# Longer runs for the q and k loads, and a new count of filler products, in an attention-then-GLU kernel

## Chip, cores, metric

One NeuronCore of one Trainium2 chip. The metric is the device time of one execution in microseconds (us), the median of several; lower is better.

## The reference, cut

```python
qn = q / (norm(q, axis=1) + 1e-6); kn = k / (norm(k, axis=1) + 1e-6)   # q, k, v: [4, 6016, 256] f32
a  = softmax(kn.transpose(0, 2, 1) @ qn / tau)                          # [4, 256, 256]
x  = (v @ a).reshape(24064, 256)
out = (sigmoid(x @ w_gate) * (x @ w_val)) @ w_out                       # d_ff = 1536
```

"Head" here means one of the four batch entries. Its 256 x 256 attention matrix needs all of its q and k before anything can be done with v.

## The kernel before

Each head has 6016 rows, 47 per partition. The kernel folds the attention matrix into the weights (`gh`: G = a @ w_gate, H = a @ w_val), so v only has to be transposed and multiplied by G and H. While the PE does this for one head, the q and k of the next are loaded, squared and scored as side work. Only head 0 has nothing to hide behind. All q, k, v and weights are cast from f32 to bf16 by the DMA and issued by POOL, in one queue (q0 in the profile); the transposes of v and the stores of the output are issued by SP, in another (q1). A chunk of v is four rows per partition, like a group of q and k; its products with G and H come in twelve slots. A filler product is one whose result nobody reads.

```python
TPC = 4                                  # rows per partition in one load
groups = [(0, 4), (4, 4), ..., (40, 4), (44, 3)]
qkpool = pool("qkpool", NCH)             # 12 buffers of 4 rows, for q and for k

def load_qk(b, t0, nt):
    for name, src in (("q", q), ("k", k)):
        tl = qkpool.tile([P, TPC, C], BF16, tag=name, name=name + "_sb")
        nc.gpsimd.dma_start(out=tl[:, :nt, :], in_=rows(src, b)[:, t0 : t0 + nt, :])
    ...
# head 0: rows 0-3 as f32 through SP and ACT, then load_qk for 4-7, 8-11, ..., 40-43, 44-45, 46,
# then v chunk 0, three pieces each of w_gate and w_val, v chunk 1, w_out
for g, (t0, nt) in enumerate(groups0):   # head 0
    ...                                  # squares on DVE and ACT, sums on DVE
    for u in range(nt):
        score(0, t0, u)
    if g < n_acc:                        # n_acc = 9: rows 0 to 35
        busy(5)                          # filler products: nobody reads their result
    ...                                  # norm products
# side work for head n, in slots of one 128-wide part of the hidden layer, 12 to a chunk of v
for g, (t0, nt) in enumerate(groups):
    s0 = first + g * (last - first) // NCH
    at(max(0, s0 - 20), load_qk, n, t0, nt)
    ...
# v of chunk ci + 2 is loaded at slot 0 of chunk ci, chunk ci + 1 is transposed at slot 2:
nc.sync.dma_start_transpose(out=vT[:, : nt * CB, :], in_=flat)   # chunks 0 and 1 of head 0: on the PE
```

## Time and profile before

| | before |
|---|---|
| time | 831.2 us (830.94 to 831.69, 6 runs) |
| PE busy | 816.1 us of a span of 829.0 |
| transfers on the chain that ended last | up to 37.3 us, then none |
| loads of q, k | 96, of 128 packets of data each |

The page gives the busy time of each engine and the chain of work that ended last. As the PE is busy 98% of the time, the chain is what to read: it says that only the first 37 us are set by something else. The lines are in the prediction.

### The profile page before, as it was taken

How to read it: one execution, taken by the hardware profiler on the slowest of the kernel's cores; microseconds unless marked ns; L12 is line 12 of the kernel's file. 1: busy time of each engine (PE TensorE's matmuls, PEld its weight loads, DVE VectorE, ACT ScalarE, POOL GpSimd, SP SyncE). 2: the span in 40 equal slices, each digit the busy share in tenths (PEclk: the TensorE clock that was granted, in tenths of full speed). 3: DMA queues.
4: the chain of work that ended last, by engine and by line, in shares of the span. 5: the costliest groups of instructions: out<-in, count | busy, mean ns of one | idle time of the engine just before them, and what ended most of it. 6: DMA issues, size and time to landing. Idle time of an engine off the chain costs nothing.

```text
span 829.0 us, 13765 instructions
## 1 busy us (share of the span) xinstructions
PE 816.1 (98%) x5192; PEld 502.6 (61%) x5206; DVE 588.9 (71%) x1022; ACT 391.6 (47%) x644; POOL 83.1 (10%) x159
## 2 busy tenths in 40 slices
PE   7899999999999999999999999999999999999998
PEld 4556666665665666665575666666566566666666
DVE  6577777887667777778767777777766666666664
ACT  4654444446644444445654444444655444444442
POOL 5531100002120100000211010000000000000000
PEclk9999999999999999999999999999999999999999
DMA  9999623226946433223875352223323423322111
GB/s 209 207 206 207 113 52 86 57 60 131 159 87 124 96 85 60 57 52 84 156 140 126 81 105 59 51 63 75 64 62 63 72 52 87 67 48 73 43 36 71
DMA packets 78739, 77.17 MB, mean 93 GB/s; under 512 B 50769, under 2 KB 55633, under 8 KB 78673
## 3 DMA queue, kind: packets, MB, share of 16 engines
q0 software_dynamic: 23920, 38.81, 28.3%
q1 hardware_dynamic: 54608, 36.97, 17.6%
q8 instruction: 40, 0.66, 0.3%
q10 hardware_dynamic: 144, 0.52, 0.2%
q14 instruction: 27, 0.21, 0.1%
HBM read 78.64 MB, written 24.64 MB: 125 GB/s over the span
## 4 chain that ended last, share of the span: by engine, by line
PE 94%; DMA 4%; DVE 1%; issue 0%; POOL 0%; ACT 0%; POOLq 0%; ACTq 0%
PE ps_o L88 30%; PE ps_gate L88 29%; PE ps_val L88 29%; PE ps_s L88 4%; DMA q_sb<-in_q_dram 3%; PE ps_gh L88 2%; DMA w_val<-in_moe_w_val_dram 1%; DVE hT L423 0%; ACT g_sb L422 0%; DVE sq L176 0%; PE ps_n L88 0%; POOL k_sb L97 0%; POOL q_sb L97 0%; PE ps_tp L393 0%; DVE out_sb L449 0%
## 5 line engine op out<-in xcount | busy, mean ns | idle before, releaser
L423 DVE TENSOR_TENSOR hT<-ps_val,g_sb 128x512 bf16<-128x512 f32 (+1 forms) x576 | 391.2, 680 | 206.3 <-ACT g_sb L422 201.9
L422 ACT ACTIVATE g_sb<-ps_gate 128x512 bf16<-128x512 f32 (+1 forms) x576 | 338.1, 588 | 386.0 <-PE ps_gate L88 380.0
L88 PE MATMUL ps_gate<-vT,gh_G 128*128 128x512 bf16 (+1 forms) x1152 | 337.6, 375 | 0.6 <-ACT g_sb L422 0.4
L88 PE MATMUL ps_val<-vT,gh_H 128*128 128x512 bf16 (+1 forms) x1152 | 337.4, 375 | 0.4
L88 PE MATMUL ps_o<-w_out_sb,hT 128*128 128x256 bf16 x2256 | 326.2, 273 | 0.0
L88 PEld LDWEIGHTS <-hT 128*128 128x128 bf16 x2256 | 220.7, 98 | 124.8
L88 PEld LDWEIGHTS <-gh_H 128*128 128x128 bf16 x1152 | 112.7, 98 | 131.6 <-issue 1.4
L88 PEld LDWEIGHTS <-gh_G 128*128 128x128 bf16 x1152 | 112.4, 98 | 38.5 <-issue 0.6
L106 POOL DMA_DIRECT2D v_sb<-in_v_dram x48 | 25.6, 533 | 619.9 <-DMA vT<-v_sb 485.8
L449 DVE COPY out_sb<-ps_o 128x256 f32<-128x256 f32 x188 | 77.9, 414 | 13.5 <-PE ps_o L88 13.5
L88 PE MATMUL ps_s<-k_sb,q_sb 128*128 128x256 bf16 x376 | 66.0, 272 | 5.7 <-DMA k_sb<-in_k_dram 4.3
L88 PEld LDWEIGHTS <-q_sb 128*128 128x128 bf16 x376 | 36.6, 98 | 14.1 <-issue 6.3
L215 DVE TENSOR_TENSOR acc<-acc,sq 128x1024 bf16<-128x1024 bf16 (+1 forms) x66 | 44.2, 669 | 0.0
L176 DVE TENSOR_TENSOR sq<-q_sb 128x1024 bf16<-128x1024 bf16 (+2 forms) x44 | 29.4, 668 | 2.7 <-DMA q_sb<-in_q_dram 2.7
L97 POOL DMA_DIRECT2D k_sb<-in_k_dram x48 | 26.3, 549 | 16.5 <-DMA k_sb<-in_k_dram 8.9
L97 POOL DMA_DIRECT2D q_sb<-in_q_dram x48 | 26.2, 545 | 16.0 <-DMA q_sb<-in_q_dram 8.6
L176 DVE TENSOR_TENSOR sq<-k_sb 128x1024 bf16<-128x1024 bf16 (+2 forms) x34 | 22.4, 658 | 0.9 <-ACT sq L174 0.9
L376 ACT ACTIVATE gh_G<-ps_gh,rrow 128x512 bf16<-128x512 f32 x21 | 14.4, 687 | 12.7 <-PE ps_gh L88 8.8
L174 ACT ACTIVATE sq<-k_sb 128x1024 bf16<-128x1024 bf16 (+1 forms) x11 | 11.2, 1018 | 14.6 <-DMA k_sb<-in_k_dram 11.8
L88 PE MATMUL ps_busy<-ones_wide,ones_bf 128*128 128x512 bf16 x57 | 16.3, 412 | 1.7 <-DVE shift L127 1.6
L378 DVE TENSOR_SCALAR gh_H<-ps_gh,rrow 128x512 bf16<-128x512 f32 x22 | 16.4, 743 | 1.6 <-PE ps_gh L88 1.6
L472 DVE TENSOR_TENSOR acc<-acc,sq 128x1024 bf16<-128x1024 bf16 x16 | 11.1, 692 | 5.1 <-ACT sq L174 4.8
(65 smaller groups left out, 124.5 us busy)
## 6 DMA issues: line engine op xcount, KB each, us to landing
out_dram<-out_sb SPq DMA_DIRECT2D x44, 512.0 KB, 2.9
v_sb<-in_v_dram POOLq DMA_DIRECT2D x44, 256.0 KB, 3.8
q_sb<-in_q_dram POOLq DMA_DIRECT2D x43, 256.0 KB, 7.8
k_sb<-in_k_dram POOLq DMA_DIRECT2D x43, 256.0 KB, 8.5
out_dram<-out_sb SPq DMA_DIRECT2D x4, 384.0 KB, 2.5
w_gate<-in_moe_w_gate_dram POOLq DMA_DIRECT2D x3, 256.0 KB, 6.8
w_val<-in_moe_w_val_dram POOLq DMA_DIRECT2D x3, 256.0 KB, 7.4
w_out_sb<-in_moe_w_out_dram POOLq DMA_DIRECT2D x1, 768.0 KB, 12.6
```

The source lines that it names most:

```text
L88: nc.tensor.matmul(out, lhsT=lhsT, rhs=rhs, start=start, stop=stop, **kw)
L97: nc.gpsimd.dma_start(out=tl[:, :nt, :], in_=rows(src, b)[:, t0 : t0 + nt, :])
L106: nc.gpsimd.dma_start(out=v_sb[:, :nt, :], in_=rows(v, b)[:, t0 : t0 + nt, :])
L174: nc.scalar.activation(out=sq[:, :nt, :], in_=src[:, :nt, :], func=ACT.Square)
L176: engine.tensor_tensor(out=sq[:, :nt, :], in0=src[:, :nt, :], in1=src[:, :nt, :], op=ALU.mult)
L215: nc.vector.tensor_tensor(out=acc[:, :nt, :], in0=acc[:, :nt, :], in1=st[b]["sq", w][:, :nt, :], op=ALU.add)
L376: nc.scalar.activation(out=dst, in_=ps, func=ACT.Copy, scale=r)
L378: nc.vector.tensor_scalar(out=dst, in0=ps, scalar1=r, scalar2=None, op0=ALU.mult)
L422: nc.scalar.activation(out=g_sb[:, :n], in_=ps_gate[:, :n], func=ACT.Sigmoid)
L423: nc.vector.tensor_tensor(out=hts[b, ci][:, f, :n], in0=ps_val[:, :n], in1=g_sb[:, :n], op=ALU.mult)
L449: nc.vector.tensor_copy(out=out_sb[:, s, :], in_=ps)
L472: nc.vector.tensor_tensor(out=acc[w], in0=acc[w], in1=sq[w], op=ALU.add)
```

## The change

Its intent: fewer and longer DMA packets. A partition's eight rows, 8 KB of f32, come in one run in place of two, and half as many loads are issued. In head 0 the first four rows and the last eleven keep their loads, so that the end of the head is not coarser. As two groups' data now land together, five fillers per group become six, with one and two after the last pair.

```diff
-    qkpool = pool("qkpool", NCH)
+    qkpool = pool("qkpool", 8)
 ...
-            tl = qkpool.tile([P, TPC, C], BF16, tag=name, name=name + "_sb")
+            tl = qkpool.tile([P, 2 * TPC, C], BF16, tag=name, name=name + "_sb")
             nc.gpsimd.dma_start(out=tl[:, :nt, :], in_=rows(src, b)[:, t0 : t0 + nt, :])
             tiles.append(tl)
-        qk[b, t0] = tiles
+        for u in range(0, nt, TPC):
+            qk[b, t0 + u] = [tl[:, u : u + TPC, :] for tl in tiles]
 ...
+    pairs = [(t, 2 * TPC) for t in range(TPC, head - 3 * TPC, 2 * TPC)]
+    loads0 = pairs + [(t, n) for t, n in groups0 if t >= pairs[-1][0] + 2 * TPC]
 ...
-            busy(5)
+            busy(6 if t0 < pairs[-1][0] else 1 if t0 == pairs[-1][0] else 2)
 ...
-            at(max(0, s0 - 20), load_qk, n, t0, nt)
+            if g % 2 == 0:
+                at(max(0, s0 - 20), load_qk, n, t0, min(2 * TPC, NT - t0))
```

More of the change, by code (lines that the diff above doesn't have):

```diff
@@ L110 @@
     t0, nt = groups0[0]
-    qk[0, 0] = [qkpool.tile([P, TPC, C], BF16, tag=n, name=n + "_sb") for n in ("q", "k")]
+    qk[0, 0] = [
+        qkpool.tile([P, 2 * TPC, C], BF16, tag=n, name=n + "_sb")[:, :TPC, :] for n in ("q", "k")
+    ]
     first_f32 = [consts.tile([P, nt, C], FP32, name=f"first{w}") for w in range(2)]
@@ L115 @@
     nc.scalar.preload_act_table(ACT.Sqrt)
-    load_qk(0, *groups0[1])
+    pairs = [(t, 2 * TPC) for t in range(TPC, head - 3 * TPC, 2 * TPC)]
+    loads0 = pairs + [(t, n) for t, n in groups0 if t >= pairs[-1][0] + 2 * TPC]
+    load_qk(0, *loads0[0])
     ident_bf = consts.tile([P, P], BF16)
@@ L130 @@
     nc.scalar.copy(qk[0, 0][1], first_f32[1])
-    for t0, nt in groups0[2:]:
+    for t0, nt in loads0[1:]:
         load_qk(0, t0, nt)
```

## The prediction

> **What bounds the kernel now.** I read the page first, for the chain and the waits; then the chain in order of time, to see which stretch it leaves to something other than the PE; then the PE's waits after the head; then the DMA traffic and the engines' order inside the head.
>
> The page, its engine line, its DMA rates in 40 slices of 20.7 us, its queues and its chain:
>
> ```profile
> PE 816.1 (98%) x5192; PEld 502.6 (61%) x5206; DVE 588.9 (71%) x1022; ACT 391.6 (47%) x644; POOL 83.1 (10%) x159
> ...
> GB/s 209 207 206 207 113 52 86 57 60 131 159 87 124 96 85 60 57 52 84 156 140 126 81 105 59 51 63 75 64 62 63 72 52 87 67 48 73 43 36 71
> ...
> q0 software_dynamic: 23920, 38.81, 28.3%
> ...
> PE 94%; DMA 4%; DVE 1%; issue 0%; POOL 0%; ACT 0%; POOLq 0%; ACTq 0%
> ```
>
> The PE is busy 98% and has 94% of the chain. DMA has 4%, some 33 us. The reader is to see that these 4% lie in one place. The chain in order of time:
>
> ```profile
> 3.47 5.85 DMA q_sb<-in_q_dram
> 9.60 9.74 DMA q_sb<-in_q_dram
> 19.63 10.60 DMA q_sb<-in_q_dram
> 30.51 6.79 DMA w_val<-in_moe_w_val_dram
> 37.34 0.59 PE ps_gh L88 x2
> ```
>
> From about 3.5 to 37.3 us the end is set by the loading of head 0: q and k (the norms and the scores need all 47 rows of a partition), one chunk of v, the first two weight pieces. After that the PE never waits for a transfer. The PE's waits from 45 us on are this one line in all:
>
> ```profile
> PE ps_gate L88 <- ACT g_sb L422: 0.4, 1, 0.4
> ```
>
> So whatever the change does to the loads of heads 1 to 3 is hidden, unless it makes a new wait; only the first 37 us can give or lose time. Inside them the PE is not the bound. Two consecutive groups of four rows in the PE's timeline:
>
> ```profile
> 18.15 1.03 PE L88 MATMUL ps_s<-k_sb,q_sb 128*128 128x256 bf16 x8 [0.42 <-DMA k_sb<-in_k_dram]
> 19.02 1.24 PE L88 MATMUL ps_busy<-ones_wide,ones_bf 128*128 128x512 bf16 x5
> 20.63 1.03 PE L88 MATMUL ps_s<-k_sb,q_sb 128*128 128x256 bf16 x8 [0.36 <-DMA k_sb<-in_k_dram]
> ```
>
> A group comes every 2.48 to 2.53 us (starts at 13.15, 15.62, 18.15, 20.63, 23.17), the PE scores it in 0.87 (start to start), fills with products that only keep it busy, and waits for k. DVE's three operations on a group take some 1.98 us (table of windows), ACT's square 1.06.
>
> **What the Trainium skill says.** (1) "DMA: Bandwidth & Descriptors", section "Where 436 GB/s comes from": the 16 engines' way into SBUF is bounded at 435 GB/s. The trace: from 10 to 22 us the DMA moves a mean of 210 GB/s counted in the bf16 that it writes (the queue's 38.81 MB is about half of the f32 read, so bf16 bytes are what is counted); read as f32 that is 420 GB/s, 96% of that bound. (2) The same page, "Why small descriptors are slow (HBM only)": a fixed overhead of about three cycles for each packet, which matters at 256 bytes. The trace agrees that it is small here, as worked out below. (3) "Perfetto Trace Analysis", section "DMA Optimizations": going from 2 KB to 4 or 8 KB per transfer can improve throughput dramatically. In this trace a run is already 4 KB read, so I expect no such thing. (4) "TensorE: Matmul & The Clock Gate", Part 1: the clock falls to half after an idle window of about 3.4 us. The page's clock line is 9 in all slices and a wait of 1.46 us before the first score left a score's 272 ns as it was; no run here shows a longer wait.
>
> **The change part by part.**
>
> *Loads.* Of head 0, rows 4 to 35 come in 4 loads of 8 rows for q and 4 for k, in place of 8 and 8; the first four rows (f32, through the other queues) and the last eleven stay as they were. Heads 1 to 3: 6 and 6 loads in place of 12 and 12. All together 52 in place of 96. Bytes are the same.
>
> What is it worth? Count packets: 21,504 rows of partitions (128 for each of 96 q, k loads and 48 v loads, 256 for each of 6 weight pieces at two rows a partition, 1536 for w_out) and 16 for each of the 151 loads make 23,920, the page's number exactly. So one packet is one partition's run, and each of 16 engines has 8 of them per q or k load plus one small one. Rates by run length, bf16 side: runs of 2048 bytes 2.51 us a pair of loads, 1.255 a load; runs of 1024 bytes (weights, 34.5 to 43 us) 205 GB/s, so 262,144 bytes in 1.279 us; runs of 512 bytes (w_out, 43 to 47 us) 204 GB/s. From the first two, 8 more packets on each engine cost 0.024 us: about 3 ns a packet. For the small packet at the end of a load: a load of 1.255 us, less 524,288 bytes at the skill's 435 GB/s (1.205), less 8 x 3 ns, leaves about 25 ns. (From the w_out rate I would get 65 ns, but then the data alone would run at 450 GB/s, above the bound; I don't take it.)
>
> Saved on each engine in head 0: 64 packets x 3 ns = 0.19 us, and 8 loads x 25 ns = 0.20 us. Sum 0.4 us. All of it lies on the path, for every later transfer up to the w_val piece that lands at 37.3 moves up by it. If the longer run got exactly the bound, rows 4 to 35 would gain 16 x (1.255 - 1.205) = 0.8 us; that is the most that I can see.
>
> *Grain.* Pair 0 is whole at the moment when, before, the third group was: 10.6 us. Nothing is lost by that at the end, as the last three pieces (rows 36, 40, 44 and 46) keep their size. But two groups' work now comes at once every 5.0 us. PE: 2 x (0.87 + 6 x 0.215) = 4.3 us, fits. DVE: 2 x 1.98 = 4.0, fits. Last pair, landed at T: PE 0.87 + 0.215 + 0.87 + 2 x 0.215 = 2.4 us, just under the 2.5 until the next k. That is what the filler cut is for; with five fillers it would be 3.9 and rows 36 would start 1.4 late. Fillers: 7 x 6 + 1 + 2 = 45, before 9 x 5 = 45; the PE work is the same. DVE for the last pair: the sum with k of rows 28 waits for ACT's square until T + 1.1, then four operations end at about T + 3.9, the next square of q at T + 4.5. The norm products behind rows 36 then end at about T + 5.0, when rows 40 land. Tight, worth 0 to 0.1 us.
>
> *Buffers.* 8 of 8 rows for 12 of 4. Head 0 takes 9, so the ninth (row 46) takes that of the first four rows, which are read by 8 to 9 us, long before. Heads 1 to 3 take 6 each, and a buffer is used again eight later, at least 60 slots of the FFN after its last reader. Loads of head 1: k of the first pair lands after 1 MB in place of 0.5 MB, 2.5 us later: before it was issued at 39.1 and landed by 51.9 at the latest (12.8, the largest time to landing), so about 54.4; its first score stands at 57.87. Hidden.
>
> Sum: 831.2 - 0.4, with up to 0.1 given back: 830.8.
>
> **The rivals.**
>
> *The skill's "dramatic" gain.* Longer runs give a few per cent of 25 us. For: it is the change's evident intent. Against: 210, 205 and 204 GB/s for runs of 2048, 1024 and 512 bytes show a flat curve. At the very most 0.8 us: 830.4.
>
> *The grain becomes the bound.* DVE falls behind the last pair, or the PE does, and norms and sqrt come later. For: the slack is 0.1 us. Against: the w_val wait hides some 0.2 us of it: the product with w_val could have begun at 36.88 + 0.22 = 37.10 and began at 37.34. Cost 0.3 to 0.8 us: 831.3 at worst.
>
> *One slow engine.* Between 23.17 and 26.53 us the scores came 3.36 apart, 0.85 more than the others, while the mean rate did not fall. In 23 to 25 us stands one packet of the queue called instruction:
>
> ```profile
> q0 software_dynamic: 220, 0.41, 109.4%
> q8 instruction: 1, 0.02, 2.9%
> ```
>
> 2.9% of 16 engines in 2 us is 0.93 us of one engine; a load is whole when its slowest engine is, so all later loads stayed late by that. If in the changed kernel this packet falls elsewhere, or two fall on one engine, the time moves by up to 0.9 us either way for a reason that has nothing to do with the run length. I give that the widest part of the range. The PE's count of instructions is the same, so most likely the packet stays.
>
> *A cold clock.* The PE waits 1.7 us for pair 0 (scores and six fillers end at about 8.9, k at 10.6) where it had none. Half of the skill's window, so I expect nothing; if cold, some 10 products at double time, 1 us, and it would be caught up before the next pair.
>
> **Range and chances.** Center 830.8, from 0.4 of gain. Low 829.8: the 0.8 and a kinder place of the instruction packet. High 831.7: no gain and 0.5 lost in the grain or with the packet. Two per cent would be 16.6 us, half of the whole head: faster 0.005, slower 0.005.
>
> **What would show it.** Right: scores in pairs 4.9 to 5.0 us apart (4.97 with my 0.4 over eight groups); 10 to 20 us at 211 to 213 GB/s; 64 x 16 fewer packets in the head and 44 x 128 + 44 x 16 = 6336 fewer in all (23,920 to 17,584); the first w_val product some 0.4 us earlier than 37.34; PE waits from 45 us on unchanged. Wrong: the pair's interval at 5.0 with the same rate (no gain); the product with e later than the w_val landing (the grain bounds); waits for k of heads 1 to 3; a score of over 272 ns after 10 us (the clock).

## The result, and the profile after

The changed kernel takes 831.0 us (830.87 to 831.25, 6 runs), the one before 831.21 us in the same rounds. The ratio is 0.9997, with an interval of 0.9985 to 1.001. (A ratio is the mean time of one kernel's fast runs over that of the other's of the same rounds, so not quite the ratio of the medians.) The time is in the range, but it says little: a gain of 0.2 us cannot be told from none. The profile says much more, for it shows both a gain and a loss.

The page of the changed kernel, the lines that answer to those of before:

```profile
PE 816.3 (98%) x5192; PEld 502.6 (61%) x5206; DVE 588.2 (71%) x1022; ACT 391.2 (47%) x644; POOL 59.8 (7%) x115
...
q0 software_dynamic: 17584, 38.80, 27.3%
...
PE 90%; DMA 7%; POOL 1%; DVE 1%; issue 0%; ACT 0%; POOLq 0%
```

17,584 packets are the number forecast. The PE does the same work. But the transfers' share of the chain has grown from 4% to 7%, although the head got shorter. The PE's timeline of the changed kernel shows the shorter head: two pairs, each of two groups, and the first product with w_val:

```profile
15.41 1.03 PE L88 MATMUL ps_s<-k_sb,q_sb 128*128 128x256 bf16 x8 [0.40 <-DMA k_sb<-in_k_dram]
...
17.58 1.04 PE L88 MATMUL ps_s<-k_sb,q_sb 128*128 128x256 bf16 x8
...
20.36 1.03 PE L88 MATMUL ps_s<-k_sb,q_sb 128*128 128x256 bf16 x8 [0.45 <-DMA k_sb<-in_k_dram]
...
36.89 0.59 PE L88 MATMUL ps_gh<-w_val,e_sb 128*128 128x512 bf16 x2
```

Pairs are 4.95 us apart (5.01 before, from 15.62 to 20.63), and the product that stood at 37.34 us before is at 36.89: 0.45 us gained. Yet the span is 829.0 us in both. The chain of the changed kernel in order of time shows where it went; the columns are start, length, and what:

```profile
35.87 12.60 DMA v_sb<-in_v_dram
48.47 0.02 issue
48.49 22.27 DMA vT<-v_sb
70.76 0.04 issue
70.80 0.60 PE ps_gate L88 x2
```

After the head the chain runs through v chunk 2 and its transpose, which lands at 70.76 us, and the PE starts on that chunk at 70.80. In the kernel before, the PE came to it at 70.88 with no wait:

```profile
70.88 0.59 PE L88 MATMUL ps_gate<-vT,gh_G 128*128 128x512 bf16 x2
```

The PE's waits of the changed kernel from 45 us on (total, times, longest) have one line more than before:

```profile
PE ps_gate L88 <- ACT g_sb L428: 0.4, 1, 0.4
PE ps_gate L88 <- DMA vT<-v_sb: 0.2, 1, 0.2
```

The transpose was issued at 48.97 before and at 48.49 after, as SP's timelines show, so 0.48 earlier. From issue to landing it took 16.2 us before and 22.3 after:

```profile
48.97 1.34 SPq L390 DMA_TRANSPOSE vT<-v_sb  x1
```

```profile
48.49 1.35 SPq L396 DMA_TRANSPOSE vT<-v_sb  x1
```

```profile
DMA to landing us min/median/max: 16.2/16.2/16.2
```

```profile
DMA to landing us min/median/max: 22.3/22.3/22.3
```

(The landing lines are those of tile vT between 40 and 72 us, of before and after.) Before, it landed near 65.2 us, with 5.7 us to spare.

**An account that adds up.** In each kernel here with no wait in between, chunk 2 starts 33.53 to 33.56 us after the first product with w_val, and the last 40 output products start 749.85 to 749.93 us after chunk 2, whatever the kernel. From there to the end of the span are 8.22 to 8.26 us, except in e6 and e7 (8.60 in both; see there). So, but for these two, the time is the start of the w_val product, plus any wait up to chunk 2, plus a constant. Before: 37.34 + 0. After: 36.89 + 0.38 (70.80 - 36.89 - 33.53) = 37.27. (The wait counted from starts, 0.38, is longer than the 0.2 of the page, which takes the modelled end of the last product.) The gain of 0.45 and the loss of 0.38 leave 0.07 us in the profiled executions.

**Theory.** The transposes and the loads share the 16 DMA engines from two queues. The Trainium skill, "DMA: Bandwidth & Descriptors", section "Queues, rings and completion order", says that an engine takes from the queues that have work in turn, packet by packet. If so, each small packet of the transpose (1024 of 256 bytes in all, so 64 on each of 16 engines) waits for one packet of the loads, which is now twice as long. The DMA traffic from 56 to 62 us (queue, packets, MB, share of engines; q0 is POOL's loads, q1 SP's transposes and stores), of before and of after:

```profile
q0 software_dynamic: 583, 1.06, 94.4%
q1 hardware_dynamic: 584, 0.15, 18.0%
```

```profile
q0 software_dynamic: 385, 1.13, 96.3%
q1 hardware_dynamic: 388, 0.10, 12.0%
```

One to one in both, as the page's taking of turns would have it; with nearly the same bytes of loads, a third fewer turns for the transpose. (A third and not a half: v's loads, which are among them, keep the short runs, and the small packet at the end of a load takes a turn too.) **Rivals:** the transpose is late because more is queued ahead of it or in another order; or the gain in the head and the wait are accidents of one profile.

### The profile page after: what moved, and what is told of

It reads as the page before. It is cut to its first block, busy times and chain, and to the rows that moved or that the text cites. A ratio compares the mean times of both kernels' runs of the same rounds, so it can differ in the third digit from the quotient of the medians.

```text
span 829.0 us, 13681 instructions
## 1 busy us (share of the span) xinstructions
PE 816.3 (98%) x5192; PEld 502.6 (61%) x5206; DVE 588.2 (71%) x1022; ACT 391.2 (47%) x644; POOL 59.8 (7%) x115
## 3 DMA queue, kind: packets, MB, share of 16 engines
q0 software_dynamic: 17584, 38.80, 27.3%
q1 hardware_dynamic: 54608, 36.97, 17.8%
## 4 chain that ended last, share of the span: by engine, by line
PE 90%; DMA 7%; POOL 1%; DVE 1%; issue 0%; ACT 0%; POOLq 0%
PE ps_o L88 29%; PE ps_gate L88 28%; PE ps_val L88 28%; PE ps_s L88 4%; DMA k_sb<-in_k_dram 3%; DMA vT<-v_sb 3%; PE ps_gh L88 2%; DMA v_sb<-in_v_dram 2%; DVE hT L429 0%; POOL w_val L145 0%; POOL w_gate L145 0%; DVE sq L182 0%; ACT g_sb L428 0%; POOL w_out_sb L150 0%; PE ps_n L88 0%
## 5 line engine op out<-in xcount | busy, mean ns | idle before, releaser
L182 DVE TENSOR_TENSOR sq<-k_sb 128x1024 bf16<-128x1024 bf16 (+2 forms) x34 | 22.4, 658 | 0.9 <-ACT sq L180 0.9
L88 PE MATMUL ps_busy<-ones_wide,ones_bf 128*128 128x512 bf16 x57 | 16.6, 418 | 1.7 <-DVE shift L133 1.6
L98 POOL DMA_DIRECT2D k_sb<-in_k_dram x26 | 14.2, 545 | 15.6 <-DMA k_sb<-in_k_dram 8.7
L98 POOL DMA_DIRECT2D q_sb<-in_q_dram x26 | 14.3, 550 | 13.3 <-DMA q_sb<-in_q_dram 7.2
```

The source lines that it names most:

```text
L88: nc.tensor.matmul(out, lhsT=lhsT, rhs=rhs, start=start, stop=stop, **kw)
L182: engine.tensor_tensor(out=sq[:, :nt, :], in0=src[:, :nt, :], in1=src[:, :nt, :], op=ALU.mult)
```

## The experiments

The column "w_val" is the start of the first product with w_val, "wait" the PE's extra time from there to chunk 2 of v (over 33.53), whatever it waited for: the transpose of chunk 2, except in e8 and e10, where the transpose was in time and a later piece of w_val was not, and in 0.7 us of e6; "transpose" is the transpose's time to landing. All three are from one profile of each run; then the medians of the timed runs, in the rounds shared with the kernel before.

| run | w_val | wait | transpose | time | before | ratio (interval) |
|---|---|---|---|---|---|---|
| before | 37.34 | 0 | 16.2 | | | |
| after | 36.89 | 0.38 | 22.3 | 831.00 | 831.21 | 0.9997 (0.9985 to 1.001) |
| a0_after | 36.97 | 0.70 | 22.6 | 831.11 | 831.01 | 1.0 (0.9986 to 1.0013) |
| e1_head0_only | 36.96 | 0 | 15.9 | 830.57 | 831.01 | 0.9993 (0.9981 to 1.0006) |
| e2_heads123_only | 37.26 | 0.46 | 22.4 | 831.43 | 831.01 | 1.0004 (0.9992 to 1.0017) |
| e4_short_runs | 37.24 | 0 | 16.6 | 830.92 | 831.01 | 0.9998 (0.9985 to 1.001) |
| e5_six_fillers | 38.57 | 0 | 22.5 | 832.14 | 831.18 | 1.0012 (0.9996 to 1.0029) |
| e6_runs16 | 36.90 | 3.18 | 24.8 | 834.91 | 831.18 | 1.0045 (1.003 to 1.006) |
| e7_loads16_runs4 | 37.14 | 0 | 16.8 | 831.10 | 831.18 | 0.9999 (0.9984 to 1.0014) |
| e8_runs1 | 38.91 | 0.80 | 16.0 | 833.27 | 830.97 | 1.0027 (1.0015 to 1.004) |
| e9_runs2 | 37.88 | 0 | 16.0 | 831.54 | 830.97 | 1.0006 (0.9993 to 1.002) |
| e10_loads2 | 38.65 | 0.92 | 15.8 | 833.13 | 830.97 | 1.0026 (1.0013 to 1.0039) |

Only for e6, e8 and e10 does the interval leave out 1. The arguments for the small ones rest on the trace, where the two terms of each are seen apart. All results were correct.

### a0_after: the changed kernel again

No edit; on one chip with e1, e2 and e4.

> The changed kernel once more, beside the others on one chip. All theories: 831.0 us, 0.2 under before; the first product with w_val starts near 36.9 us (before: 37.34), and the products of v chunk 2 start near 70.8 us (before: 70.88), after a wait for its transpose. If the gain of 0.45 us in the head or the wait at 70.8 came from where an instruction packet fell, one of the two should not come back.

Both came back: 36.97 us in the head, and a wait, this time of 0.70 us. Its profiled run took 831.33 us, and the median, 0.1 above before, is no gain at all. So the changed kernel's end is set by the landing of the transpose (70.76 us in one profile, some 71.2 in the other), and no longer by the head.

### e1_head0_only: long runs in head 0, short in the others

```diff
-            if g % 2 == 0:
-                at(max(0, s0 - 20), load_qk, n, t0, min(2 * TPC, NT - t0))
+            at(max(0, s0 - 20), load_half, n, t0, nt)   # 4 rows into one half of a tile of 8
```

> Head 0 as in the changed kernel; heads 1 to 3 again in loads of four rows, two into each tile of eight. Packet theory (the transpose of v chunk 2 sends some 64 small packets on each DMA engine, and each waits behind one packet of the loads' queue, which is twice as long with runs of eight rows): the transpose takes 16 us again in place of 22.3, lands near 65 us, the wait at 70.8 us is gone, and the whole 0.45 us of the head stays: 830.75. Rival that the head's gain is lost elsewhere or is noise: 831.0 to 831.2, whatever the transpose does.

Measured 830.57 us, 0.44 under before; its five runs lie from 830.52 to 830.60, the nine of before from 830.83 to 831.42. From 45 us on the PE's waits are those of before, the transpose took 15.9 us, and the traffic from 56 to 62 us has its old count again:

```profile
q0 software_dynamic: 584, 1.07, 93.9%
q1 hardware_dynamic: 583, 0.15, 18.0%
```

The head's gain stays as soon as the other heads' runs are short. This version is the fastest here, by 0.05%: every run of it is under every run of both kernels, though the interval of the ratio still takes in 1.

### e2_heads123_only: the other half

```diff
+    loads0 = groups0[1:]                 # head 0 as before, four rows a load
-            busy(6 if t0 < pairs[-1][0] else 1 if t0 == pairs[-1][0] else 2)
+            busy(5)
```

> Head 0 as before (loads of four rows, five fillers); heads 1 to 3 in loads of eight. Packet theory: first w_val product near 37.34 us as before; the transpose of v chunk 2 takes 22 us, lands near 71.2 us, later than the 70.4 to 70.9 us at which it is wanted, so the PE waits some 0.4 us: 831.5, slower than before. Rival that only the head matters: 831.2.

831.43 us, 0.42 over before, where 831.5 was expected: the part of the change that was to be hidden costs, by itself, as much as the other part gains. The w_val product stands at 37.26 and chunk 2 starts at 71.25, in the PE's timeline:

```profile
71.25 0.60 PE L88 MATMUL ps_gate<-vT,gh_G 128*128 128x512 bf16 x2 [0.30 <-DMA vT<-v_sb]
```

### e4_short_runs: the same loads, packets of the old length

```diff
-            tl = qkpool.tile([P, 2 * TPC, C], BF16, ...)
-            nc.gpsimd.dma_start(out=tl[:, :nt, :], in_=...)
+            tl = qkpool.tile([P, 2, TPC + 1, C], BF16, ...)      # a gap after each four rows
+            nc.gpsimd.dma_start(out=tl[:, :, :TPC, :], in_=...)  # (the load of seven rows as two)
```

> Loads of eight rows in the same order as in the changed kernel, but each partition's eight rows are written as two runs of four with a gap, so that packets have their old length. Packet theory: transpose of v chunk 2 16 us again, no wait at 70.8 us. Rival (the amount or the order of what is queued delays the transpose): 22 us and the wait stays. In the head it parts the two terms of my sum: half as many loads but as many packets should keep only the 0.2 us of the packets at the end of a load, so the first w_val product near 37.1 us; with the packet theory the time is 831.0, with the rival 831.2.

The transpose took 16.6 us and the wait is gone, though order and amounts are those of the changed kernel, and so are the loads but for those of seven rows:

```profile
DMA to landing us min/median/max: 16.6/16.6/16.6
```

So it is the length of the run that delays the transpose, not what is queued. In the head only 0.1 us of the gain is left (37.24).

### e6_runs16 and e7_loads16_runs4: a larger dose, and its control

Rows 8 to 23 of head 1 come in one load of 16 rows; in e7 the tile has a gap after each four rows.

```diff
+    tl = attp.tile([P, 4, TPC * C + PAD], BF16, ...)     # PAD: 0 in e6, 16 in e7
+    nc.gpsimd.dma_start(out=tl[:, :, : TPC * C], in_=rows(src, b)[:, t0 : t0 + 4 * TPC, :]...)
```

> The changed kernel, but rows 8 to 23 of head 1 come as one load of 16 rows, for q and for k, so 16 packets of twice the length again on each engine. Packet theory: of the 64 small packets of the transpose, 16 then wait behind packets of four times the old length; 16 x 0.31 + 16 x 0.63 + 16 x 0.31 + 16 x 0.16 = 22.5 us and 6.2 us of its own (from before: 16.2 less 64 x 0.156): 28.7 us, landing near 77 us, some 6.5 us of PE wait, 837.5. Rival (amount queued): nearly the same bytes are queued, so 22 to 24 us and 831 to 832.

> As the one with the load of 16 rows, but its rows are written in four runs of four, so its packets have the old length. Packet theory: 16 x 0.31 + 48 x 0.16 + 6.2 = 18.9 us, landing near 67.5 us, no wait, 830.75. Rival (amount or order of what is queued): as late as with runs of 16.

With the same bytes in the same loads, e6 comes to chunk 2 3.18 us late and e7 in time: 834.91 against 831.10 us. The PE's timelines of e6 and of e7:

```profile
73.61 0.61 PE L88 MATMUL ps_gate<-vT,gh_G 128*128 128x512 bf16 x2 [2.33 <-DMA vT<-v_sb]
```

```profile
70.68 0.59 PE L88 MATMUL ps_gate<-vT,gh_G 128*128 128x512 bf16 x2
```

The rival is out. (Of the 3.18 us, 0.7 had been lost before, at a late piece of w_val whose cause I did not look for; as the transpose landed at 73.5 us, the PE would have lost them there. The profiled run is one of two short ones, 834.08 and 834.24 us; the other two took 835.59 and 835.72, for which there is no profile.) From 56 to 62 us e6 has

```profile
q0 software_dynamic: 162, 1.18, 93.9%
q1 hardware_dynamic: 164, 0.04, 5.1%
```

again one to one, and not in bunches: from 60.0 to 60.6 us it has 16 packets of each queue, as many as there are engines. 16 engines x 6 us over the number of turns gives the length of a turn on an engine: 0.165 us before (583), 0.249 after (385), 0.593 in e6 (162).

But the dose gave half of the wait that I expected, 3.18 us in place of 6.5, and 24.8 us of transpose in place of 28.7. I had let all 64 turns wait behind a load. From 68 to 74 us e6 has

```profile
q0 software_dynamic: 309, 0.81, 68.3%
q1 hardware_dynamic: 367, 0.09, 10.3%
```

so the loads' queue was running dry by then: POOL had nothing to issue from 51.67 to 74.09 us, as its next v load waited for this very transpose, and the last small packets went alone. The "6.2 us of its own" of my estimate was too much as well. In before, after and e6 alike, the first packet of the transpose moves 3.8 to 3.9 us after its issue, and it lands 0.5 to 0.9 us after its last one starts: some 4.5 us in all (read from the start times of single packets in the traces). The turns between take 11.7, 17.5 and 20.4 us, where I had expected 22.5 for e6. These two terms make up the 3.9 us that were missing.

The e7 run should have been 0.4 under before and was 0.1. Its profile shows two reasons. Its last 40 products start at 820.59 us, 0.20 before those of the kernel before, but its span ends 8.60 us after that, some 0.35 later than in the others. In e6 and e7 alone a packet of an instruction queue (q14) stands behind the last store; that it is the cause is not shown. And its w_val product stands at 37.14, although its head is that of the changed kernel. Five profiles of this head (after, a0, e1, e6, e7) give 36.89 to 37.14, mean 36.97; two of the old one (before, e2) 37.34 and 37.26, mean 37.30. So the head's gain is about 0.33 us, with a scatter of 0.25 from kernel to kernel whose cause I did not find.

### e5_six_fillers: without the filler cut

```diff
-            busy(6 if t0 < pairs[-1][0] else 1 if t0 == pairs[-1][0] else 2)
+            busy(6)
```

> The changed kernel with six fillers after every group, so without the cut for the last pair. Both groups of the last pair then hold the PE 4.3 us in place of 2.4, the scores of rows 36 start near 30.5 us (28.6 in the changed kernel) and the last norm products end 1.2 us later. Of this some 0.25 us is hidden behind the w_val landing, and some 0.4 us behind the wait for the transpose at 70.8 us: 831.6, with the first w_val product near 37.8 us and no wait for the transpose. If the PE were not on the path at the end of head 0, 831.0 and 36.9 us.

Measured 832.14 us and the w_val product at 38.57: the cut is needed, and is worth more than I thought, 1.6 us in the head (38.57 - 36.97) and about 1.0 in the time, as the wait for the transpose vanishes: chunk 2 starts at 72.13 us, after the transpose has landed. The scores of rows 36 start at 30.77 us (28.60 in the changed kernel) and the last norm products end 1.4 us later. What I missed, as I read the timeline, came next. There are two buffers of squares, and with the norm products late, the squares wait for them; no run with more buffers tests this. ACT's timeline of e5:

```profile
34.13 0.42 ACT L180 ACTIVATE sq<-q_sb 128x256 bf16<-128x256 bf16 x1 [0.77 <-PE ps_n L88]
```

In the changed kernel this square followed the one before it at 33.00 with no wait.

### e8_runs1, e9_runs2, e10_loads2: what a packet and a load cost in the head

From the kernel before, rows 4 to 43 of head 0: the same loads written in runs of one row (e8) or two (e9), by gaps in the tile; or loads of two rows (e10).

```diff
-            nc.gpsimd.dma_start(out=tl[:, :nt, :], in_=rows(src, b)[:, t0 : t0 + nt, :])
+            # e8, e9: tile with a gap of 16 elements after each run of 1 or 2 rows
+            nc.gpsimd.dma_start(out=tl_with_gaps, in_=...rearrange("p (h t) c -> p h (t c)", t=run))
+            # e10:
+            for u in range(0, nt, 2):
+                nc.gpsimd.dma_start(out=tl[:, u : u + 2, :], in_=rows(src, b)[:, t0 + u : t0 + u + 2, :])
```

> The kernel before, but rows 4 to 43 of head 0 land in runs of one row (each load of four rows is written with gaps): 480 more packets on each DMA engine, as many loads. At my 3 ns a packet: the first w_val product 1.4 us later than 37.34 (38.8), 832.6. If the 0.35 to 0.45 us that the changed kernel won in the head is all packets (5 to 7 ns each): 2.4 to 3.4 us later, 833.6 to 834.6. If it is all at the ends of loads: 37.3 and 831.2.

> The same with runs of two rows: 160 more packets on each engine, as many loads. At 3 ns: 0.5 us later, 831.7. At 5 to 7 ns: 0.8 to 1.1 us, 832.0 to 832.3. All at the ends of loads: 831.2.

> The kernel before, but rows 4 to 43 of head 0 come in loads of two rows: 160 more packets and 20 more loads on each engine. It differs from the one with runs of two rows by the ends of 20 loads alone: at my 25 ns another 0.5 us (832.2); if the end of a load costs nothing, as that one. A third way: with loads half as long POOL's issue (0.53 us a load, 0.63 us of data) and the eight loads in flight may not keep the engines fed, and it is later by several us.

e8: 38.91 - 37.34 = 1.57 us for 480 packets on each engine, 3.3 ns a packet. e9: 0.54 us for 160, 3.4 ns, though on a difference only twice the scatter of 0.25 us. The DMA rate from 12 to 22 us fell in e8, from 1151 packets to 3945 in the same time; before, and e8:

```profile
DMA packets 1151, 2.10 MB, mean 210 GB/s; under 512 B 128, under 2 KB 128, under 8 KB 1151
```

```profile
DMA packets 3945, 1.96 MB, mean 196 GB/s; under 512 B 113, under 2 KB 3945, under 8 KB 3945
```

The time of e8 rose by more, 2.3 us, since a later piece of w_val was now late as well (the wait of 0.80). The profile of e8, waits of the PE:

```profile
PE ps_gh L88 <- DMA w_val<-in_moe_w_val_dram: 0.7, 1, 0.7
```

e10 does not settle what the end of a load costs. Its w_val product is 0.77 us after that of e9, which would be 38 ns for each of 20 loads; but in e10 POOL no longer waits for transfers, it issues four loads in 2.6 us with hardly a pause (POOL's waits for DMA from 8 to 24 us are 0.5 us in all, 9.4 in the kernel before). So issue may be a bound of its own there, the third way that I had named, though not by several us. What the ends cost in the changed kernel is better read from e4: half the loads, the old packets, 0.1 us.

## Why the prediction was right or wrong

**Which stretch counts: half wrong.** "Whatever the change does to the loads of heads 1 to 3 is hidden, unless it makes a new wait" left the door open, and I then looked only at who waits for q and k. Those were hidden, as I said: no wait for k after the head. The new wait was in another queue's transfer. Before had 5.7 us to spare at chunk 2, and the transpose took 6.1 us longer. The view was at hand: the traffic of both queues from 56 to 62 us, 583 against 584 packets, is in the trace of before.

**The loads' 0.4 us: right.** 0.45 in the first profile, 0.33 in the mean. The packet's 3 ns measured 3.3 and 3.4 (e8, e9), so 64 packets are 0.21 us. The curve that I called flat falls a little: from 12 to 22 us, head 0 moved 196 GB/s in runs of 512 bytes (e8), 205 in runs of 1024 (e9) and 210 in runs of 2048. My 204 for 512 bytes came from a window of which 73 of 1372 packets were longer. The end of a load, estimated at 25 ns, was somewhat high: eight of them left 0.10 us in e4, some 13 ns each, though with the scatter of 0.25 us this is no more than a size. The 25 ns rested on the 435 GB/s for the way into SBUF, which I set against the f32 that is read, 420 GB/s, while 210 GB/s of bf16 went into SBUF; no run here shows that the bound holds on the read side.

**Grain and fillers: right in kind.** Pairs fit, and the norm products behind rows 36 ended just as the scores of rows 40 began (31.07). The waits for DVE there are 0.2 and 0.2 us and cost nothing that shows. What the cut is worth I put too low before the run of e5 (0.95 us in the head, measured 1.6), probably for want of the squares' buffers.

**Buffers and clock: right.** No wait for a buffer shows; the PE's wait before pair 0 was 1.42 us in its timeline, and the scores after it took their usual 1.03 us for eight.

**The sum: the step that failed.** "831.2 - 0.4, with up to 0.1 given back" should have been 0.33 to 0.45 gained and 0.38 to 0.70 given back, so between 0.1 us gained and 0.4 lost, about nothing. That the time fell into the range was luck: both terms are small and nearly cancel, and the reason given for the center was half of the story. My sign "PE waits from 45 us on unchanged" failed, and it was the one that told.

**The instruction packet: stayed**, as thought likely. The scores in every kernel here have their long gap between 22 and 28 us, and it cannot be blamed for a difference.

## What to carry to other kernels

Before you lengthen the runs of one DMA queue, look at what else is in flight on the engines. In this kernel two queues took turns packet by packet, so longer packets in one were longer waits for the other, and a transpose of 64 small packets on each engine took 6.1 us longer. Long runs paid in head 0, where no transpose by DMA was in flight (e1), and cost beside a transpose that someone waited for (e2). A total that did not move is no sign that nothing happened: compare the same event in both traces, here the first product with w_val and the first of chunk 2, and the gain and the loss come apart.

## What the Trainium skill lacked or had wrong

- "DMA: Bandwidth & Descriptors", section "Queues, rings and completion order": its turns between queues are borne out (583 to 584, 385 to 388 and 162 to 164 packets in 6 us). It puts 9 to 17 descriptors typically into a packet; here each record of the trace that takes a turn is one partition's run, whether 2, 4 or 8 KB are written (in e6 a turn is 0.593 us, with one record of each queue). What it lacks is the consequence: doubling the runs of one queue took a transpose on the other from 16.2 to 22.3 us, with the same bytes to load.
- "Perfetto Trace Analysis", section "DMA Optimizations": going to 4 or 8 KB "can dramatically improve throughput". Here runs of 1, 2, 4 and 8 KB read gave 196 (e8), 205 (e9), 210 and 213 GB/s (before and after), counted in bf16, from 12 to 22 us: 2.4% from 2 to 4 KB and 1.4% from 4 to 8.
- "DMA: Bandwidth & Descriptors", section "Why small descriptors are slow (HBM only)": a fixed cost per packet, given in cycles. Measured here: 3.3 to 3.4 ns a packet on each engine, for runs of 1 and 2 KB read, far above the 256 bytes of its example.
- "Runtime: NRT & Kernel Launch" would be the place for what a packet of the instruction queue does to the loads in flight; no page that I read says it. Here one packet of the instruction queue (16 KB, 0.93 us of one engine) falls into the gap where scores come 3.36 us apart in place of 2.5, between 23.17 and 26.53 us. No run took it away, so that it holds up the later loads is argued and not shown.
